# Attention into a dense pair on one core: all loads uncast in one ordered queue, casts on the engines, q and k as 96 rows of 6 tokens, pooling from the transposed copies

## Chip, cores, metric

The kernel runs on one NeuronCore of a Trainium2 chip. The metric is device time in microseconds (us), smaller is better. Times are medians over several executions; the kernel before takes 394.83 us (394.24 to 395.02, three runs).

Engine names: PE is the matmul engine (PEld its weight loads), DVE the vector engine, ACT the scalar engine, POOL the GpSimd engine, SP the engine that here only issues DMAs.

## The reference, cut to what matters

```python
# q, k, v: (8 batches, 8 heads, 576 tokens, 64), fp32; w_in (512, 2048), w_out (2048, 512)
q_d = q.reshape(B, H, 144, 4, D).mean(axis=3)       # the same for k_d, v_d
out_d = softmax(q_d k_d^T / 8) v_d                  # 144 x 144 scores
out_up = repeat(out_d, 4, axis=tokens)
out_local = softmax(mask(q k^T / 8)) v              # mask: |i - j| < 4
x = (out_up + out_local) as (4608 tokens, 512)
h = x @ w_in
out = (h - tanh(h)) @ w_out                         # fp32
```

For each head, q and k are needed twice: token by token, with the head dimension on the partitions, for a band of local scores, and averaged over groups of 4 tokens for the pooled scores. The attention output feeds two dense products, which are most of the PE's work.

## The kernel before

Words used below. A *pair* is two heads of one batch (128 columns of x). There are 32 pairs, four a batch. A *dense block* is 512 tokens of x; there are 9, each with 16 groups of four w_in matmuls (`mm1`) and 16 groups of four w_out matmuls (`mm2`). Block 0 needs all four pairs of batch 0, and so the first dense matmul cannot start before those four pairs are done.

The order of instructions on every engine is fixed when the kernel is built. Each step is recorded as an `op(engine, modelled ns, function, reads, writes, pri)`, and a list scheduler plays the steps through a model with those durations and emits them in the order that the model started them. Engines then run in that order.

```python
# scheduler, the choice of the next step on each engine
now = max(free.get(eng, 0.0), min(at[i] for i in cand))
pick = min((self.ops[i][4], i) for i in cand if at[i] <= now)[1]   # lowest pri first
# [cut]

def load_qk(p):                       # two casting DMAs a pair, issued by POOL: 128 rows of 4 tokens
    # [cut]
            GP.dma_start(out=qkn[s][:, i, hh:hh + 2],               # bf16 <- fp32 in DRAM
                in_=src[b, h0:h0 + 2, 0:512, :].rearrange("h (g a) d -> g h (a d)", a=4))
def load_tail(b):                     # tokens 512..575 of all heads: two more casting DMAs a batch
    # [cut]
def load_v(p):                        # fp32, SP's queue; windows of 128 tokens every 120 tokens
    # [cut]                           # rows of 64 floats (256 bytes)
def load_w(src, dst, name, f, pri):   # weights: four casting DMAs each, issued by POOL
    # [cut]
def prep_v(p):                        # POOL casts v into vw
    # [cut]

def attention(p):
    for i in range(2):                # DVE: put the tokens of q, k in order for the transposes
        op("DVE", 240, ...)           # qr <- qkn, bf16
    op("POOL", 1100, add1, ...)       # pooling on the loaded rows: a sum of token pairs,
    op("POOL", 650, add2, ...)        # then of the two sums
    def tr():                         # PE, one PSUM tile `ps`
        # 8 transposes 128x128, 1 transpose of the tail,
        # 2 matmuls for pooled q, k, and 1 that pools the tail
    # readers of that PSUM tile: ACT 512 columns of q, ACT 512 of k, ACT tails,
    #                            DVE pooled k (kd), ACT pooled q (qd)
    op("PE", 400, s1, reads=qks, writes=ts, pri=pri)   # first scores, into the same PSUM tile
    # [cut] exp, mask multiply, second scores (local window 4 and pooled), outputs, xT

def dense(kb):                        # kb 0: all mm1, then all mm2; kb 1: all mm1;
    # [cut]                           # then mm1 of block kb interleaved with mm2 of block kb - 1
```

The softmax here doesn't subtract the row's maximum and nothing guards it: scores larger than these inputs give would overflow.

Of the kernel before, what the change touches and what calls it, by code (L numbers as in the profile page):

```python
# [15 lines left out]
class Program:  # L16
# [34 lines left out]
    def order(self):  # L51
# [12 lines left out]
        for _ in range(n):  # L64
            best = None
            for eng, cand in ready.items():
                if not cand:
                    continue
                now = max(free.get(eng, 0.0), min(at[i] for i in cand))
                pick = min((self.ops[i][4], i) for i in cand if at[i] <= now)[1]  # L70
                if best is None or now < best[0]:
                    best = (now, eng, pick)
# [21 lines left out]
def kernel(  # L94
# [17 lines left out]
    SCALE = 1.0 / float(D) ** 0.5  # L112
    QW = 120
# [16 lines left out]
    NQKN, NVST, NVW = 3, 2, 3  # L130
    W_IN_PRI, W_OUT_PRI = -25, 0
# [7 lines left out]
    qkn = fixed("qkn", [128, 2, 4, 256], BF16, NQKN)  # L139
    tl = fixed("tl", [128, H * D], BF16, 2)  # L140
    vst = fixed("vst", [128, 4, NT, 64], FP32, NVST)
    vw = fixed("vw", [128, 4, NT, 65], BF16, NVW)
    vd = fixed("vd", [128, 2, 4, 65], BF16, NVW)
    qr = fixed("qr", [128, 2, 4, 128], BF16, 2)
    sm1 = fixed("half", [128, 2, 2, 128], BF16)
    sm = fixed("sm", [128, 2, 128], BF16, 2)
    qk = fixed("qk", [128, 1192], BF16, 2)
    qd = fixed("qd", [128, G], BF16, 2)
    kd = fixed("kd", [128, G], BF16, 2)
# [70 lines left out]

    def load_qk(p):

        b, h0, s = p // NP, 2 * (p % NP), (p // 2) % NQKN
        for i, src in enumerate((q, k)):
            key = ("qkn", s, p % 2, i)

            def issue(i=i, src=src):
                hh = 2 * (p % 2)
                GP.dma_start(
                    out=qkn[s][:, i, hh:hh + 2],  # L230
                    in_=src[b, h0:h0 + 2, 0:512, :].rearrange(
                        "h (g a) d -> g h (a d)", a=4))
            op("POOL", 700, issue, writes=[key, ("q", key)], pri=10 * p - 60)
            op("DMA", 1300, None, reads=[("q", key)], writes=[key],
               pri=10 * p - 60)

    def load_tail(b):
        for i, src in enumerate((q, k)):
            key = ("tl", b % 2, i)

            def issue(i=i, src=src):
                GP.dma_start(
                    out=tl[b % 2][64 * i:64 * i + 64, :].rearrange(
                        "p (h d) -> p h d", d=D),
                    in_=src[b, :, 512:576, :].rearrange("h p d -> p h d"))
            op("POOL", 750, issue, writes=[key, ("q", key)], pri=40 * b - 60)
            op("DMA", 1200, None, reads=[("q", key)], writes=[key],
               pri=40 * b - 60)

    def load_v(p):  # L250
        b, j = p // NP, p % NP
        hb = p // 2
        for hh in range(2):
            h, i = 2 * j + hh, 2 * (p % 2) + hh
            t = vst[hb % NVST]
            key = ("vst", hb % NVST, i)

            def win(tok, n, nt, base=v[b, h]):
                return bass.AP(tensor=base.tensor, offset=base.offset + tok * D,
                               ap=[[D, n], [QW * D, nt], [1, D]])  # L260

            def issue(h=h, i=i, t=t, win=win):
# [8 lines left out]
            if (b, h) in ((0, 0), (B - 1, H - 1)):  # L271
                def clear(h=h, i=i, t=t):
                    part = t[0:32, i, 0, :] if h == 0 else t[96:128, i, 4, :]
                    V.memset(part, 0.0)
                op("DVE", 100, clear, writes=[key], pri=-9)
            op("SP", 900, issue, writes=[key, ("q", key)], pri=10 * p - 55)
            op("DMA", 900, None, reads=[("q", key)], writes=[key], pri=10 * p - 55)

    def load_w(src, dst, name, f, pri):
        def issue():  # L280
            if src is moe_w_in:
                GP.dma_start(out=dst[:, :, 512 * f:512 * f + 512],
                             in_=src[:, 512 * f:512 * f + 512].rearrange(
                                 "(c p) f -> p c f", p=128))
            else:
                GP.dma_start(out=dst[:, 4 * f:4 * f + 4, :],
                             in_=src.rearrange("(f p) n -> p f n", p=128)
                             [:, 4 * f:4 * f + 4, :])
        key = (name, f)
        op("POOL", 800, issue, writes=[key, ("q", key)], pri=pri)  # L290
        op("DMA", 4500, None, reads=[("q", key)], writes=[key], pri=pri)


    def prep_v(p):
        hb, jj = p // 2, p % 2
        s, w = hb % NVST, hb % NVW
        pri = 10 * p - 52
        op("POOL", 650, lambda: GP.tensor_copy(
            out=vw[w][:, 2 * jj:2 * jj + 2, :, 0:64],
            in_=vst[s][:, 2 * jj:2 * jj + 2]),  # L300
           reads=[("vst", s, 2 * jj), ("vst", s, 2 * jj + 1)],
           writes=[("vw", w, jj)], pri=pri)

    def pool_v(hb):
# [11 lines left out]
        op("PE", 660, mm, reads=[("vw", w, 0), ("vw", w, 1), "pick"],  # L316
# [7 lines left out]
    def attention(p):  # L324
        b, j, hb, s, jj = p // NP, p % NP, p // 2, p % 2, p % 2
        tb, sn, w = b % 2, hb % NQKN, hb % NVW
# [4 lines left out]
        src = qkn[sn][:, :, 2 * jj:2 * jj + 2, :]  # L331


        for i in range(2):
            op("DVE", 240, lambda i=i: V.tensor_copy(  # L335
                out=qr[s][:, i].rearrange("p a (h d) -> p h a d", d=D),
                in_=src[:, i].rearrange("p h (a d) -> p h a d", d=D)),
               reads=[("qkn", sn, jj, i)], writes=[("qr", s, i)], pri=pri)

        def add1():  # L340
            with nc.allow_low_precision("pooled q and k"):
                GP.tensor_tensor(out=sm1, in0=src[:, :, :, 0:128],
                                 in1=src[:, :, :, 128:256], op=ALU.add)

        def add2():
            with nc.allow_low_precision("pooled q and k"):
                GP.tensor_tensor(  # L347
                    out=sm[s].rearrange("p i (h d) -> p i h d", d=D),
                    in0=sm1[:, :, :, 0:64], in1=sm1[:, :, :, 64:128], op=ALU.add)
        op("POOL", 1100, add1, reads=[("qkn", sn, jj, 0), ("qkn", sn, jj, 1)],  # L350
           writes=["sm1"], pri=pri - 57)
        op("POOL", 650, add2, reads=["sm1"], writes=[("sm", s)], pri=pri - 57)


        b16 = ps[:, 0].bitcast(BF16)
        t16 = ps[:, 1, 0:64].bitcast(BF16)
        g32 = ps[:, 1, 64:352]

        def tr():
            for i in range(2):  # L360
                for a in range(4):
                    c = 512 * i + 128 * a
                    T.transpose(b16[:, c:c + 128], qr[s][:, i, a, :], ident)  # L363
            tail = tl[tb][:, 128 * j:128 * j + 128]
            T.transpose(t16, tail, ident)
            for i in range(2):
                T.matmul(g32[:, G * i:G * i + 128], sm[s][:, i, :], ident,
                         start=True, stop=True)
            T.matmul(g32.rearrange("p (i g) -> p i g", i=2)[:, :, 128:144], tail,  # L369
                     group, start=True, stop=True)  # L370
        op("PE", 680, tr,
           reads=[("qr", s, 0), ("qr", s, 1), ("tl", tb, 0), ("tl", tb, 1),
                  ("sm", s), "ident", "group"], writes=ts, pri=pri)
        full = bass.AP(tensor=qk[s].tensor, offset=qk[s].offset,
                       ap=[qk[s].ap[0], [KOFF, 2], [1, 576]])
        for i in range(2):
            op("ACT", 480, lambda i=i: A.copy(  # L377
                out=full[:, i, 0:512].rearrange("p (g a) -> p g a", a=4),
                in_=b16[:, 512 * i:512 * i + 512].rearrange(
                    "p (a g) -> p g a", a=4)),  # L380
               reads=ts, writes=[("qk", s, i)], pri=pri)
        op("ACT", 170, lambda: A.copy(
            out=full[:, :, 512:576], in_=t16.rearrange("p (i c) -> p i c", i=2)),
           reads=ts, writes=[("qk", s, 2)], pri=pri)
        op("DVE", 230, lambda: V.tensor_copy(out=kd[s], in_=g32[:, G:2 * G]),
           reads=ts, writes=[("kd", s)], pri=pri)
        op("ACT", 190, lambda: A.activation(  # L387
            out=qd[s], in_=g32[:, 0:G], func=AF.Copy, scale=1.0 / 16.0),
           reads=ts, writes=[("qd", s)], pri=pri)
# [15 lines left out]
        def s2():  # L405
            for hh in range(2):
                score(4, hh, 128 + 384 * hh)
            for i in range(2):
                for hh in range(2):
                    rows = slice(64 * hh, 64 * hh + 64)  # L410
                    c = 224 + 384 * hh + G * i
                    T.matmul(sc[:, c:c + G], kd[s][rows, 16 * i:16 * i + 128],
                             qd[s][rows, :], start=True, stop=True)
        qks = [("qk", s, i) for i in range(3)]
        op("PE", 400, s1, reads=qks, writes=ts, pri=pri)
# [225 lines left out]
```

## Time and profile before

| | before |
|---|---|
| time, median | 394.83 us |
| span of the profiled run | 392.6 us |
| PE busy | 348.9 us (89%) |
| POOL busy | 151.0 us, 35.5 of it in the first 43 us |
| first dense matmul starts at | 43.1 us |
| software (casting) DMA / hardware DMA | 13.64 MB / 19.92 MB |

The page of the profile cuts the span into 40 slices of 9.8 us; a digit is the busy share of an engine in tenths. These are the rows of PE, POOL and PE's granted clock, and the two DMA queues:

```profile
...
PE   1466798976996899999999999999999999999996
...
POOL 8996654454769556645555322310000000000000
PEclk9997599998999799999999999999999999999999
...
q0 software_dynamic: 30080, 13.64, 28.2%
q1 hardware_dynamic: 47150, 19.92, 18.9%
...
```

PE is full from the fifteenth slice on, some 140 us; before that it has holes. POOL is the busiest engine of the first slices.

The same by stretches of the span. In each line: the stretch and its length, then the busy time and instruction count of each engine, the granted PE clock, the share of busy DMA engines and what they moved.

```profile
...
core 0: us, PE busy (x) PEld busy (x) DVE busy (x) ACT busy (x) POOL busy (x), PEclk, DMA share, GB/s
0.00:43.00 43.00, 19.59 (x216) 15.01 (x217) 21.76 (x50) 16.42 (x31) 35.49 (x59) 0.90 1.11 172
43.00:140.00 97.00, 83.54 (x749) 47.82 (x761) 63.34 (x118) 61.50 (x118) 58.70 (x74) 0.92 0.73 119
140.00:400.00 260.00, 245.72 (x1872) 128.70 (x1903) 143.85 (x251) 143.86 (x273) 56.79 (x71) 1.00 0.26 58
...
```

Span is PE's busy time plus its idle time, so PE's idle time says where the rest is: 43 - 19.59 = 23.4 us up to 43 us, 97 - 83.54 = 13.5 us between 43 and 140 us, and 252.6 - 245.72 = 6.9 us after it. (45 of 2,880 matmul records are missing in this trace. Between 43 and 140 us there are 12 fewer matmuls than weight loads, so at 0.216 us each idle time may be overstated there by 2.6 us.)

What POOL does in the first microseconds, in order of time (start, duration, engine, line, operation, tiles):

```profile
...
1.33 0.87 POOL L229 DMA_DIRECT2D qkn_71<-in_q_dram  x1 [0.81 <-POOLq L625]
...
2.91 0.72 POOL L242 DMA_DIRECT2D tl_74<-in_q_dram  x1
3.60 0.71 POOL L242 DMA_DIRECT2D tl_74<-in_k_dram  x1
...
6.19 0.73 POOL L229 DMA_DIRECT2D qkn_71<-in_k_dram  x1
7.08 1.17 POOL L342 TENSOR_TENSOR half<-qkn_71 128x512 bf16<-128x512 bf16 x1 [0.17 <-DMA qkn_71<-in_k_dram]
8.33 0.66 POOL L347 TENSOR_TENSOR sm_87<-half 128x256 bf16<-128x256 bf16 x1
...
9.59 0.61 POOL L207 TENSOR_SCALAR_AFFINE_SELECT mask<-mask 128x480 bf16<-128x480 bf16 x1
...
```

Each casting load costs POOL 0.7 to 0.9 us of issue, and pooling and the mask stand in line behind those. PE's first steps show what that does (in brackets the idle time before an instruction and what ended it):

```profile
...
9.70 0.26 PE L365 MATMUL ps_ts<-ident,tl_74 128*128 128x128 bf16 x1 [1.78 <-DMA tl_74<-in_k_dram]
...
12.34 0.58 PE L397 MATMUL ps_ts<-qk_89 64*128 64x120 bf16 x8 [2.14 <-ACT qd_91 L387]
...
43.10 0.58 PE L499 MATMUL ps_hy_497<-xT_65,w_in_sb 128*128 128x512 bf16 x1 [1.16 <-DVE xT_68 L479]
...
```

Eight transposes of pair 0 are through before 8 us, but the ninth, of the tail, waits for its tile until 9.70 us. Then the first scores wait 2.14 us, because they write the PSUM tile that five copies have to leave first; the pooled q (`qd`) is the last of the five. This wait comes again: in the whole span PE waits 8.2 us for `qd`.

```profile
...
PE ps_ts L397 <- ACT qd_91 L387: 4.5, 3, 2.1
...
PE ps_ts L397 <- ACT qd_92 L387: 3.7, 3, 2.1
...
```

### The profile page before, as it was taken

To read this page: it belongs to the slowest core of one execution; us is meant where nothing else is said; L and a number is where in the kernel's file an instruction comes from. 1 tells how busy PE (TensorE), PEld (TensorE's weight loads), DVE (VectorE), ACT (ScalarE), POOL (GpSimd) and SP (SyncE) were. 2 spreads that over 40 slices of the span, in tenths; PEclk is the share of its full clock that TensorE was granted. 3 is DMA by queue.
4 is the path that set the end of the run, shared out by engine and by line. 5 is a ranking of instruction groups with operands and counts; after the bars stand their busy time and mean duration, and the time that the engine had idled before them with its cause. 6 is when DMAs were issued, how large, how long until landed. Compare 5 with 4: busy or idle time off the path is not lost.

```text
span 392.6 us, 7296 instructions
## 1 busy us (share of the span) xinstructions
PE 348.9 (89%) x2835; PEld 191.5 (49%) x2880; DVE 228.9 (58%) x417; ACT 221.8 (56%) x421; POOL 151.0 (38%) x203
## 2 busy tenths in 40 slices
PE   1466798976996899999999999999999999999996
PEld 0345344444554565555655556555554444444442
DVE  3374487316897587777677766776644443343410
ACT  1536286364885677776776776767744444434421
POOL 8996654454769556645555322310000000000000
PEclk9997599998999799999999999999999999999999
DMA  9699993466759648568554400000010010101012
GB/s 158 126 185 209 203 186 63 60 116 128 130 92 154 116 64 139 95 132 138 96 110 69 66 29 23 33 2 28 28 53 28 28 53 28 53 27 45 37 53 80
DMA packets 77264, 34.02 MB, mean 87 GB/s; under 512 B 52142, under 2 KB 72622, under 8 KB 77230
## 3 DMA queue, kind: packets, MB, share of 16 engines
q0 software_dynamic: 30080, 13.64, 28.2%
q1 hardware_dynamic: 47150, 19.92, 18.9%
q8 instruction: 22, 0.36, 0.4%
q14 instruction: 12, 0.10, 0.1%
HBM read 37.74 MB, written 9.44 MB: 120 GB/s over the span
## 4 chain that ended last, share of the span: by engine, by line
PE 80%; ACT 8%; DVE 8%; issue 2%; DMA 2%; POOL 1%; ACTq 0%; DVEq 0%; POOLq 0%
PE ps_hy_497 L499 8%; PE ps_hy_498 L524 8%; PE ps_hy_499 L499 8%; PE ps_hy_499 L524 8%; PE ps_hy_500 L499 8%; PE ps_hy_500 L524 7%; PE ps_hy_497 L524 7%; PE ps_hy_498 L499 7%; PE ps_ts L397 3%; PE ps_ts L363 3%; PE ps_ox L444 2%; PE ps_ox L312 2%; ACT qk_89 L377 2%; ACT qk_90 L377 2%; PE ps_ox L474 2%
## 5 line engine op out<-in xcount | busy, mean ns | idle before, releaser
L499 PEld LDWEIGHTS <-w_in_sb 128*128 128x128 bf16 x576 | 53.8, 99 | 63.2 <-issue 6.1
L524 PEld LDWEIGHTS <-gT_103 128*128 128x128 bf16 x320 | 29.2, 97 | 32.7
L524 PEld LDWEIGHTS <-gT_104 128*128 128x128 bf16 x256 | 24.0, 98 | 27.1
L377 ACT COPY qk_89<-ps_ts 128x512 bf16<-128x512 bf16 x32 | 17.7, 591 | 25.6 <-PE ps_ts L369 24.6
L377 ACT COPY qk_90<-ps_ts 128x512 bf16<-128x512 bf16 x28 | 15.5, 590 | 15.8 <-PE ps_ts L369 14.1
L524 PE MATMUL ps_hy_498<-w_out_sb,gT_103 128*128 128x512 bf16 x79 | 20.0, 379 | 0.0
L524 PE MATMUL ps_hy_500<-w_out_sb,gT_103 128*128 128x512 bf16 x78 | 19.6, 379 | 0.4 <-issue 0.3
L524 PE MATMUL ps_hy_497<-w_out_sb,gT_103 128*128 128x512 bf16 x75 | 19.5, 379 | 0.3
L524 PE MATMUL ps_hy_499<-w_out_sb,gT_103 128*128 128x512 bf16 x76 | 19.4, 379 | 0.2
L347 POOL TENSOR_TENSOR sm_88<-half 128x256 bf16<-128x256 bf16 x16 | 11.2, 701 | 19.8 <-PE ps_ts L369 18.8
L347 POOL TENSOR_TENSOR sm_87<-half 128x256 bf16<-128x256 bf16 x16 | 12.0, 747 | 17.8 <-PE ps_ts L369 16.8
L363 PE MATMUL ps_ts<-ident,qr_84 128*128 128x128 bf16 x128 | 11.0, 234 | 7.6 <-DVE qr_84 L335 6.7
L460 DVE TENSOR_TENSOR ln_99<-ps_ox,r_97 128x896 bf16<-128x896 f32 x16 | 17.4, 1086 | 0.3
L416 ACT ACTIVATE E_95<-ps_ts 128x960 bf16<-128x960 f32 x16 | 15.6, 976 | 3.4 <-PE ps_ts L397 3.4
L420 DVE TENSOR_TENSOR E_95<-E_95,mask 128x960 bf16<-128x960 bf16 x16 | 12.4, 776 | 8.2 <-ACT E_95 L416 8.0
L416 ACT ACTIVATE E_96<-ps_ts 128x960 bf16<-128x960 f32 x14 | 13.6, 974 | 6.1 <-PE ps_ts L397 6.1
L397 PE MATMUL ps_ts<-qk_89 64*128 64x120 bf16 (+1 forms) x160 | 9.9, 219 | 7.7 <-ACT qd_91 L387 4.5
L524 PE MATMUL ps_hy_500<-w_out_sb,gT_104 128*128 128x512 bf16 x61 | 15.8, 379 | 0.4 <-issue 0.2
L524 PE MATMUL ps_hy_498<-w_out_sb,gT_104 128*128 128x512 bf16 x62 | 16.0, 379 | 0.1
L524 PE MATMUL ps_hy_497<-w_out_sb,gT_104 128*128 128x512 bf16 x61 | 15.9, 379 | 0.1
L524 PE MATMUL ps_hy_499<-w_out_sb,gT_104 128*128 128x512 bf16 x60 | 15.6, 379 | 0.3 <-issue 0.3
L460 DVE TENSOR_TENSOR ln_100<-ps_ox,r_98 128x896 bf16<-128x896 f32 x14 | 15.2, 1087 | 0.3
(227 smaller groups left out, 964.8 us busy)
## 6 DMA issues: line engine op xcount, KB each, us to landing
vst_76<-in_v_dram SPq DMA_DIRECT2D x31, 160.0 KB, 3.0
vst_77<-in_v_dram SPq DMA_DIRECT2D x31, 160.0 KB, 4.3
out_dram<-y_108 SPq DMA_DIRECT2D x12, 256.0 KB, 2.1
out_dram<-y_109 SPq DMA_DIRECT2D x12, 256.0 KB, 2.0
out_dram<-y_110 SPq DMA_DIRECT2D x12, 256.0 KB, 2.0
w_in_sb<-in_moe_w_in_dram POOLq DMA_DIRECT2D x4, 512.0 KB, 8.9
w_out_sb<-in_moe_w_out_dram POOLq DMA_DIRECT2D x4, 512.0 KB, 12.5
qkn_71<-in_q_dram POOLq DMA_DIRECT2D x12, 128.0 KB, 3.4
```

Of the source, the lines that this page charges most:

```text
L312: T.matmul(pv[:, 0, :], pick[:, t, :], vw[w][:, :, t, 0:64], start=(t == 0), stop=(t == NT - 1))
L347: GP.tensor_tensor(out=sm[s].rearrange("p i (h d) -> p i h d", d=D), in0=sm1[:, :, :, 0:64], in1=sm1[:, :, :, 64:128], op=ALU.add)
L363: T.transpose(b16[:, c:c + 128], qr[s][:, i, a, :], ident)
L377: op("ACT", 480, lambda i=i: A.copy(out=full[:, i, 0:512].rearrange("p (g a) -> p g a", a=4), in_=b16[:, 512 * i:512 * i + 512].rearrange( ...
L397: T.matmul(sc[:, c:c + NQ[t]], qk[s][rows, k0:k0 + 128], qk[s][rows, QW * t:QW * t + NQ[t]], start=True, stop=True)
L416: op("ACT", 870, lambda: A.activation(out=E[s][:, 0:960].rearrange("p (h c) -> p h c", h=2), in_=ps[:, :, 0:480], func=AF.Exp, scale=SCALE ...
L420: op("DVE", 760, lambda: V.tensor_tensor(out=E[s][:, 0:960].rearrange("p (h c) -> p h c", h=2), in0=E[s][:, 0:960].rearrange("p (h c) -> p ...
L444: T.matmul(po[:, hh, 65 * t:65 * t + 65], E[s][:, c:c + 128], vw[w][:, 2 * jj + hh, t, :], start=True, stop=True)
L460: op("DVE", 1010, lambda: V.tensor_tensor(out=ln[s].rearrange("p n (h d) -> p h n d", d=D), in0=blocks[:, :, :, 0:64], in1=r[s].unsqueeze( ...
L474: T.transpose(px[0][:, QW * t:QW * t + n], ln[s][0:n, t, :], ident[0:n, 0:n])
L499: T.matmul(ps_hy[slot], w_in_sb[:, dc, fc * 128:(fc + 1) * 128], xT[dc][:, kb * 512:kb * 512 + 512], start=(dc == 0), stop=(dc == N_DC - 1))
L524: T.matmul(ps_hy[slot], gT[g][:, fc, ts * 128:ts * 128 + 128], w_out_sb[:, fc, :], start=(fc == 0), stop=(fc == N_FF - 1))
```

## The change

Its intent: take the 88 load issues off POOL, start earlier, and give PE less to do in each pair.

1. All loads go uncast (fp32) through SP's one hardware queue, in the order of the program. The Trainium skill ("DMA: Bandwidth & Descriptors", SWDGE vs HWDGE vs iDMA) says that a DMA that casts has to be issued by GpSimd; the two queue lines above agree with it, 13.64 MB. So the casts move to engines.
2. q and k are loaded as 96 rows of 6 tokens. That covers all 576 tokens, and the tail goes. 12 transposes of 96 columns replace 9 of 128 and 3 pooling matmuls.
3. Pooling reads the transposed copies `qk` (DVE in batch 0, POOL after it).
4. The weights are staged as fp32 in buffers that are idle early (gT, and xT's later half) and cast by POOL, ACT and DVE.
5. Eight of block 0's sixteen `mm2` groups are kept as filler for block 1.

The diff, cut to its core:

```diff
+                if eng == "DMA":                      # the queue serves in order of arrival
+                    pick = min((at[i], i) for i in cand)[1]
+    def load(ns, fn, keys, cost, pri):
+        op("SP", ns, fn, writes=list(keys) + ["queue", ("q", keys[0])], pri=pri)
+        op("DMA", cost, None, reads=[("q", keys[0])], writes=keys, pri=pri)
     def load_qk(p):
-                GP.dma_start(out=qkn[s][:, i, hh:hh + 2],
-                    in_=src[b, h0:h0 + 2, 0:512, :].rearrange("h (g a) d -> g h (a d)", a=4))
-            op("POOL", 700, issue, ...)
+                nc.sync.dma_start(out=qkn[s][:, i], in_=src[b, h0:h0 + 2].rearrange(
+                        "h (g a) d -> g h (a d)", a=A6))            # A6 = 6
+            load(500, issue, [("qkn", s, i)], T_QK, -30)
-    def load_tail(b): [cut]
     def load_v(p):
+            load(1000, issue, [("vst", s, i)], T_V, -30)
     def load_w(...):
+        load(600, issue, keys, T_W, -30)                            # fp32 into idle buffers
+        for c in range(4):
+            op(eng, ns, lambda ...: fn(out=to, in_=part), ...)      # casts: POOL, ACT, POOL, DVE
     def attention(p):
+            op(eng, ns, ... fn(out=dst, in_=srt) ...)    # reorder and cast: DVE, and ACT or POOL
+                for a in range(A6):
+                    T.transpose(b16[:, G6 * a:G6 * a + G6], qr[s][:, i, a, :], ident[0:G6, 0:G6])
-        # tail transpose, pooling matmuls, copies of kd and qd
+        op(e2, ..., half <- four[..., 0:2] + four[..., 2:4], reads=[("qk", s, 0), ("qk", s, 1)])
+        op(e2, ..., qkd <- half[..., 0] + half[..., 1])
     def dense(kb):
+            for i in range(M2_FIRST): mm2(kb, i)         # the other 8 go between block 1's mm1
+    M2_FIRST = 8
+    T_QK, T_V, T_W, W_PRI, NEARLY = 1000, 550, 2900, -3, NP
```

`T_QK` and `T_V` are the modelled times of one q or k load and of one v load.

## The prediction

> **What bounds the kernel now.** From about 140 us it is TensorE: busy time by stretches gives 245.7 of 249 us between 140 and 389. The losses are early. From 0 to 43.1 us, when the first dense matmul starts (timeline of PE), PE is busy only 19.6 us, at half pace; the chain of waits there runs through DVE, ACT, POOL and a DMA. Between 43 and 140 us PE idles another 13 us, at a clock of 0.93 and 0.91. The timeline shows why: POOL is busy 35.5 of the first 43.1 us, issuing cast-loads (0.73 us each), pooling (1.16 + 0.7 us a pair) and building the mask. Pair 0 waits for the tail tile until 9.7 us; the first PSUM copy is at 10.2, the first exp at 13.0. While POOL works, DVE's reorder copies grow from 0.28 to 0.75-1.44 us.
>
> **What the change does.**
> - Takes 88 load issues from POOL. The Trainium skill ("DMA: Bandwidth & Descriptors", SWDGE vs HWDGE vs iDMA) says a cast in a DMA must take the GpSimd path; so casts move to engines. POOL gains, per later pair, a k reorder (estimate 0.9 us, from the 640-element cast at 0.75) and pooling that now follows the copies (estimate 1.3 + 0.8, scaled by size): 2 us of new latency before the second scores, which dense work should hide.
> - PE: 12 transposes of 96 columns replace 9 of 128 and 3 pooling matmuls: 0.65 us a pair (warm) becomes an estimated 0.52, 4 us in all, on the critical path.
> - ACT: two copies of 576 (estimate 0.65 each) replace 1.77 us. DVE: one reorder of 0.8 replaces 1.0 plus a 0.31 cast. In the first batch DVE takes the pooling (1.1 us a pair) and ACT the k reorder (0.74).
> - 32 weight casts of about 0.5 us, 16 inside the first batch, at fixed places of in-order engines: late weights block attention behind them.
> - q0 can land near 4 us instead of 5.5, and no tail is waited for: the first PSUM copy near 6, not 10.2.
>
> **Sum.** With four pairs of about 13 us chain, two at a time, and DVE and ACT needing some 24 and 20 us for the first batch, I expect the first dense matmul at 34 us (30 to 38) instead of 43: 9 us. PE work saves 4 us. Bubbles and half-pace stretches between 43 and 140 us (about 20 us lost) should shrink by 5 to 7, because loads run ahead and half of dense block 0's second matmul is kept as filler. Total about 19 us: **375 us**, range **365 to 386**. Chances: faster by over 2% 0.90, within 2% 0.07, slower 0.03.
>
> **What would show it.** First dense matmul before 38 us; first exp near 8-9; no software DMA traffic in the queue table; transposes at 0.042 us each when warm; first w_out matmuls near 53 us instead of 65; PE idle in the first stretch down by 8-10 us; from 140 us still over 98% PE.
>
> **What would make it wrong.** (1) The one queue is slower than I think: 8 MB of fp32 weights are ordered between batches. At 250 GB/s w_in lands at 35 us and w_out at 66, casts block ACT and DVE, and most of the gain goes; v's 256-byte rows issued at about 1 us each under load before, so this is the main risk. (2) DVE and POOL still slow each other. (3) The longer pooling chain stalls PE where there is little dense work. (4) The order is fixed by modelled durations; where they are off, an engine waits. If everything flows as planned, the first dense matmul comes at 29 us and the time is near 366.

## More of the kernel before

A wrong modelled duration costs nothing by itself, but the order that it leads to is obeyed: an instruction whose data is late holds up all instructions behind it on its engine.

## The result

| | before | after |
|---|---|---|
| time, median (range), four runs each | 394.92 us (394.24 to 396.2) | 379.69 us (378.52 to 380.0) |
| span of the profiled run | 392.6 us | 378.2 us |
| PE busy | 348.9 us | 342.2 us |
| POOL busy | 151.0 us | 114.6 us |
| first dense matmul | 43.1 us | 36.1 us |
| first w_out matmul | 65.4 us | 59.8 us |

The ratio is 0.9605 (95% interval 0.9573 to 0.9637). Here and below a ratio is the mean time of one kernel's fast runs over that of the kernel before in the same rounds, so it is not quite the ratio of the medians that are quoted.

The lines of the page that answer to those of before, with the row of DMA rates, one number a slice:

```profile
...
PE   2675989849999999999999999999999999999995
...
POOL 5144565445345433445434543223000000000000
PEclk9965899978999999999999999999999999999999
...
GB/s 195 238 384 209 193 366 242 206 212 264 152 99 160 140 151 125 127 127 141 159 149 127 126 125 30 30 28 29 29 28 32 53 28 56 29 28 57 28 55 83
...
q1 hardware_dynamic: 64782, 47.19, 51.0%
...
```

The software queue is gone. In its first ten slices the rate row has two kinds: 366 to 384 GB/s where a weight passes, and some 190 to 270 in the slices of q, k and v. The stretches:

```profile
...
0.00:43.00 43.00, 25.21 (x254) 16.39 (x256) 26.67 (x61) 24.67 (x42) 18.08 (x37) 0.80 1.10 249
43.00:140.00 97.00, 86.19 (x838) 47.88 (x849) 64.68 (x109) 64.12 (x120) 46.54 (x58) 0.96 0.86 201
140.00:400.00 260.00, 230.76 (x1744) 119.82 (x1775) 130.74 (x204) 133.37 (x240) 50.03 (x57) 1.00 0.24 67
...
```

PE's idle time is now 17.8 us up to 43 us, 10.8 us between 43 and 140 us, and 238.2 - 230.76 = 7.4 us after it. So the 14.4 us of span come from PE's busy time (6.7), its first 43 us (5.6) and the stretch to 140 us (2.7); after 140 us nothing is won (0.6 is lost). Of the 6.7 us, some 3.9 are saved work (see below); where the rest comes from was not traced.

The early part is mended as meant: pair 0's transposes start at 4.36 us and the first scores at 8.01 us, after 0.73 us of waiting for a copy.

```profile
...
4.36 0.66 PE L341 MATMUL ps_ts<-ident,qr_87 96*128 96x96 bf16 x6 [4.36 <-DVE qr_87 L330]
...
8.01 0.58 PE L371 MATMUL ps_ts<-qk_89 64*128 64x120 bf16 x8 [0.73 <-ACT qk_89 L345]
...
```

Two spots are not. The first is the start of the dense work:

```profile
...
33.99 0.66 PE L341 MATMUL ps_ts<-ident,qr_87 96*128 96x96 bf16 x6 [0.95 <-DVE qr_87 L330]
35.66 0.66 PE L341 MATMUL ps_ts<-ident,qr_87 96*128 96x96 bf16 x6 [1.01 <-POOL qr_87 L330]
36.12 0.63 PE L473 MATMUL ps_hy_519<-xT_65,w_in_sb 128*128 128x512 bf16 x1
...
```

The last xT of batch 0 ended at 34.6 us (33.86 + 0.74), but the transposes of pair 4, of the next batch, stand ahead of the dense matmuls in PE's order and wait twice for their data, about 1 us each. So the first dense matmul comes at 36.12 us, 1.5 us late. It also starts at half clock: until 39.66 us the dense matmuls start 0.43 us apart and the granted clock is 0.50. Those of the kernel before start 0.43 us apart too, from 43.10 us on.

The second is larger, at 80 us. PE, then POOL, in order of time:

```profile
...
80.26 0.22 PE L371 MATMUL ps_ts<-qk_89 64*128 64x96 bf16 x2
84.14 0.42 PE L386 MATMUL ps_ts<-qkd_92 64*128 64x144 bf16 x4 [3.66 <-POOL qkd_92 L360]
84.49 0.61 PE L473 MATMUL ps_hy_521<-xT_65,w_in_sb 128*128 128x512 bf16 x1
84.89 0.64 PE L473 MATMUL ps_hy_521<-xT_66,w_in_sb 128*128 128x512 bf16 x1
...
```

```profile
...
80.75 0.72 POOL L291 CAST vw_83<-vst_80 128x640 bf16<-128x640 f32 x1 [3.63 <-DMA vst_80<-in_v_dram]
81.41 0.82 POOL L330 CAST qr_87<-qkn_73 96x768 bf16<-96x768 f32 x1
82.20 1.14 POOL L354 TENSOR_TENSOR half<-qk_89 128x576 f32<-128x576 bf16 x1
83.42 0.67 POOL L360 TENSOR_TENSOR qkd_92<-half 128x288 bf16<-128x288 f32 x1
...
```

PE waits 3.66 us for the pooled q and k (`qkd_92`) of the current pair. POOL could have made them earlier, but in its order a cast of v (`vw_83`), for a later pair, comes first, and it waits 3.63 us for a DMA. The chain of waits confirms it: in it the wait for `vst_80` is 8.28 us long and ends at 80.62 us. After the stall, matmuls start 0.40 to 0.43 us apart instead of 0.216. The Trainium skill ("TensorE: Matmul & The Clock Gate", Part 1) says that the clock falls to half after an idle window of about 3.4 us, and gives 426.7 and 215.7 ns for 512 columns; this stall agrees with both, with a wait of 3.66 us and a granted clock of 0.50 from 84 to 88 us. But so long a wait was not needed everywhere in this trace: in the 10 us before the half-clock start at 36.12 us no wait of PE was longer than 1.47 us.

Why the DMA was late: the model gave one pair 2 x 1.0 us for q and k and 2 x 0.55 us for v, 3.1 us in all. The loads of batch 1 took about 19 us for four pairs, 4.7 us each. The queue is thus behind its schedule until about 85 us, and every instruction whose place was chosen by the model may stand too early.

### The profile page after: what moved, and what is told of

The parts are those of the page before. It is cut to its first block, busy times and chain, and to the rows that moved or that the text cites. A ratio compares the mean times of both kernels' runs of the same rounds, so it can differ in the third digit from the quotient of the medians.

```text
span 378.2 us, 7323 instructions
## 1 busy us (share of the span) xinstructions
PE 342.2 (90%) x2832; PEld 184.1 (49%) x2880; DVE 222.1 (59%) x371; ACT 222.2 (59%) x401; POOL 114.6 (30%) x151
## 4 chain that ended last, share of the span: by engine, by line
PE 65%; DMA 14%; ACT 5%; DVE 5%; SPq 4%; issue 3%; POOL 3%; POOLq 0%; ACTq 0%; DVEq 0%
PE ps_hy_519 L498 8%; PE ps_hy_521 L498 7%; PE ps_hy_519 L473 6%; PE ps_hy_521 L473 6%; PE ps_hy_522 L498 6%; PE ps_hy_522 L473 6%; PE ps_hy_520 L473 6%; PE ps_hy_520 L498 6%; DMA vst_80<-in_v_dram 5%; DMA gT_102<-in_moe_w_in_dram 3%; SPq L256 3%; PE ps_ts L341 2%; DMA qkn_72<-in_k_dram 2%; DMA gT_103<-in_moe_w_out_dram 2%; PE ps_ts L371 2%
## 5 line engine op out<-in xcount | busy, mean ns | idle before, releaser
L473 PEld LDWEIGHTS <-w_in_sb 128*128 128x128 bf16 x576 | 52.4, 99 | 58.6 <-issue 3.9
L498 PEld LDWEIGHTS <-gT_102 128*128 128x128 bf16 x320 | 30.4, 98 | 35.6
L498 PEld LDWEIGHTS <-gT_103 128*128 128x128 bf16 x256 | 24.2, 98 | 28.1
L345 ACT COPY qk_89<-ps_ts 128x576 bf16<-128x576 bf16 x32 | 19.5, 645 | 15.2 <-PE ps_ts L341 15.2
L345 ACT COPY qk_90<-ps_ts 128x576 bf16<-128x576 bf16 x28 | 16.7, 643 | 9.5 <-PE ps_ts L341 9.5
L341 PE MATMUL ps_ts<-ident,qr_87 96*128 96x96 bf16 x192 | 13.0, 219 | 8.6 <-DVE qr_87 L330 5.3
L354 POOL TENSOR_TENSOR half<-qk_89 128x576 f32<-128x576 bf16 x14 | 16.6, 1189 | 8.2 <-ACT qk_89 L345 8.2
L354 POOL TENSOR_TENSOR half<-qk_90 128x576 f32<-128x576 bf16 x14 | 16.3, 1162 | 9.4 <-ACT qk_90 L345 9.4
L341 PEld LDWEIGHTS <-qr_87 96*128 96x128 bf16 x192 | 10.4, 104 | 10.3 <-DVE qr_87 L330 5.5
```

Source lines behind the costliest of these rows:

```text
L341: T.transpose(b16[:, G6 * a:G6 * a + G6], qr[s][:, i, a, :], ident[0:G6, 0:G6])
L345: op("ACT", 540, lambda i=i, b16=b16: A.copy(out=full[:, i].rearrange("p (g a) -> p g a", a=A6), in_=b16.rearrange("p (a g) -> p g a", a=A6)),
L354: op(e2, 1150 if e2 == "POOL" else 700, lambda: eng.tensor_tensor(out=half, in0=four[:, :, :, 0:2], in1=four[:, :, :, 2:4], op=ALU.add), r ...
L473: T.matmul(ps_hy[slot], w_in_sb[:, dc, fc * 128:(fc + 1) * 128], xT[dc][:, kb * 512:kb * 512 + 512], start=(dc == 0), stop=(dc == N_DC - 1))
L498: T.matmul(ps_hy[slot], gT[g][:, fc, ts * 128:ts * 128 + 128], w_out_sb[:, fc, :], start=(fc == 0), stop=(fc == N_FF - 1))
```

## The experiments

The main theory (called Q) was that the slow queue, with the order made for a faster one, took back a part of the gain. Rivals were that POOL had become too slow for pooling (P), that DVE and ACT bounded the first batch (D), that the weights' staging hurt, that the filler was what helped, and that the loads alone, or the rows and pooling alone, were the gain. One more question was how much of PE's saved work was worth time at all. All diffs are against the changed kernel, if not told otherwise.

| label | change | time, median | ratio to before | 95% interval |
|---|---|---|---|---|
| (after) | | 379.69 | 0.9605 | 0.9573 to 0.9637 |
| e1_v_long_rows | v in long rows (wrong result) | 371.11 | 0.9414 | 0.9363 to 0.9464 |
| e2_v_cast_later | v cast behind pooling | 371.98 | 0.9428 | 0.9391 to 0.9465 |
| e3_queue_as_measured | order made for 4.7 us a pair | 368.76 | 0.9348 | 0.9307 to 0.939 |
| e4_weights_cast_dma | weights by casting DMA | 375.79 | 0.9526 | 0.9485 to 0.9568 |
| e5_dense_order_old | no filler | 376.83 | 0.9526 | 0.9452 to 0.96 |
| e7_both_orders | e2 and e3 | 368.06 | 0.9328 | 0.9278 to 0.9378 |
| e8_before_uncast_qk | before, q and k uncast | 392.81 | 0.9977 | 0.9904 to 1.0049 |
| e9_four_more_transposes | PE work added | 381.2 | 0.967 | 0.9608 to 0.9733 |
| e11_long_rows_both_orders | e1 and e7 (wrong result) | 368.69 | 0.9319 | 0.926 to 0.9377 |
| e12_both_orders_old_dense | e7, no filler | 371.13 | 0.9382 | 0.9332 to 0.9432 |
| e6_before_new_dense_order | before, with filler | 397.82 | 1.0066 | 0.9997 to 1.0135 |
| e13_qk_cast_dma | e7, q and k by casting DMA | 376.25 | 0.9531 | 0.95 to 0.9562 |

### e1_v_long_rows: is the queue's rate a limit?

Its output is wrong, which doesn't matter for the time. v's rows hold other tokens than they should.

```diff
-   nc.sync.dma_start(out=t[:, i], in_=win(-4, 128, 5))          # 640 rows of 256 bytes
+   nc.sync.dma_start(out=t[:, i]....[:, 0:288],                 # 128 rows of 1,152 bytes
+       in_=bass.AP(tensor=base.tensor, offset=base.offset, ap=[[288, 128], [1, 288]]))
```

> Wrong result on purpose: v is read as 128 rows of 1152 bytes (10% fewer bytes, 4.5 times fewer rows), everything else and the engines' orders kept. Theory Q (the load queue limits the first 85 us, and the 256-byte rows of v are its slow part): q/k/v phases move well over 200 GB/s (near the 366 of the weight phases), the wait of PE for the pooled q/k at 84 us (3.7 us, plus 1.7 at half clock) goes, first dense matmul moves from 36.1 to 33 or 34, time 371 to 375. Rival P (POOL's pooling chain is too slow by itself) and rival D (DVE and ACT bound the first batch): unchanged within 1.5 us, 378 to 380.

Measured: 371.11 us, first dense matmul at 32.54 us. What the DMA queues moved from 30 to 37 us, when both kernels load only q, k and v, first in the changed kernel, then here:

```profile
...
DMA packets 2677, 1.40 MB, mean 200 GB/s; under 512 B 2115, under 2 KB 2667, under 8 KB 2676
...
```

```profile
...
DMA packets 1307, 1.65 MB, mean 235 GB/s; under 512 B 123, under 2 KB 1306, under 8 KB 1306
...
```

The rate rises, and as a pair is 885 KB here (two heads of q, k and v) it takes 3.8 us by this rate, instead of 4.7. So v's short rows held the queue back. But the expectation missed in two points: the rate is far from that of the weights, and the wait at a late v cast is still there (3.0 us, now at 75 us). This run changes the rate and, with it, every arrival, so it does not say yet whether the rate or the order is to blame.

### e2_v_cast_later: take the v cast out of the way

```diff
-           reads=[("vst", s, 0), ("vst", s, 1)],
+           reads=[("vst", s, 0), ("vst", s, 1)] + ([("qkd", p % 2)] if p > 3 else []),
 [...]
-        if p + 2 < NPAIR:
-            prep_v(p + 2)
         attention(p)
+        if p + 2 < NPAIR:
+            prep_v(p + 2)
```

The added dependency makes the model place the cast of a later v behind the current pair's pooling.

> The changed kernel, but POOL's cast of a later pair's v is placed behind the pooling of the current pair, so a late v cannot hold up pooled q/k. Loads, engines and amounts of work are the same. Theory Q with in-order blocking: the 3.7 us wait at 84 us and the half-clock stretch after it shrink by at least 3 us in all, time 374 to 377. Rival P (pooling of 1.15 + 0.67 us is itself too long): the wait stays, 378 to 380.

Measured: 371.98 us, 7.7 us less than the changed kernel and better than expected. The first dense matmul stays at 36.29 us. The stretches from 60 us show the cure:

```profile
...
60.00:80.00 20.00, 16.62 (x171) 9.47 (x172) 11.90 (x18) 9.98 (x20) 10.03 (x13) 1.00 1.19 203
80.00:100.00 20.00, 19.84 (x201) 11.36 (x203) 15.13 (x26) 15.70 (x30) 7.84 (x10) 1.00 1.16 239
...
```

PE is busy 19.84 of 20 us between 80 and 100 us. In the changed kernel that stretch reads:

```profile
...
80.00:100.00 20.00, 16.22 (x148) 8.60 (x149) 10.68 (x19) 10.92 (x20) 11.54 (x14) 0.83 0.90 207
...
```

So the stall also cost clock (0.83 against 1.00). POOL has the same work and the same speed as before the edit (busy 114.8 us, and 114.6 in the changed kernel); it only does it in another order. PE's longest wait for `qkd` falls from 3.66 to 0.9 us. This refutes P.

### e3_queue_as_measured: only a number of the model

```diff
-    T_QK, T_V, T_W, W_PRI, NEARLY = 1000, 550, 2900, -3, NP
+    T_QK, T_V, T_W, W_PRI, NEARLY = 1000, 1350, 2900, -3, NP
```

With 1.35 us a v load, the model gives a pair 2 x 1.0 + 2 x 1.35 = 4.7 us, as measured. Nothing that the chip does is changed but the order.

> The changed kernel with one constant of its scheduler changed: a v load is taken as 1350 ns instead of 550, near what the saturated queue showed (about 4.7 us for a pair's q, k and two v). Only the engines' fixed orders change. Theory Q with wrong order: the transposes of pair 4 no longer stand in front of the first dense matmul (36.1 to about 34.7), the wait at 84 us goes, time 372 to 376. If the order costs nothing (queue rate alone, or rival D): 378 to 381.

Measured: 368.76 us, 10.9 us less than the changed kernel, again more than expected. The first dense matmul:

```profile
...
32.74 0.58 PE L473 MATMUL ps_hy<-xT,w_in_sb 128*128 128x512 bf16 x1 [1.20 <-DVE xT L453]
...
```

It now waits for xT alone: it is the 217th matmul in PE's order instead of the 229th, ahead of pair 4's transposes. From 60 to 100 us PE is busy 39.25 of 40 us. Theory Q holds in this form: not the slow queue but an order made for a faster one. Rival D, which expected 378 to 380 us, falls as the reason for the lost time; what the first dense matmul still waits for, though, is DVE.

### e7_both_orders: do the two cures add up?

The edits of e2 and e3 together.

> The changed kernel with both order edits: a v load taken as 1350 ns by the scheduler, and POOL's cast of a later v behind the current pooling. Correct result. If both cure the same blocking, the time is that of the better alone, 367 to 370; if they add, 361 to 365.

Measured: 368.06 us. Alone the two were worth 7.7 and 10.9 us; together they are worth 11.6 and not 18.6, so the two largely cure the same blocking. The intervals of e3 and e7 overlap. This is the best correct version (ratio 0.9328), and not to be told from e3.

```profile
...
0.00:43.00 43.00, 26.76 (x268) 16.84 (x271) 27.72 (x63) 26.48 (x46) 17.38 (x36) 0.84 1.09 255
43.00:140.00 97.00, 92.23 (x952) 53.48 (x967) 72.63 (x120) 71.23 (x135) 56.34 (x64) 0.96 0.98 218
140.00:400.00 260.00, 220.14 (x1616) 112.98 (x1643) 119.14 (x190) 123.08 (x223) 45.74 (x52) 1.00 0.21 60
...
```

PE's idle time between 43 and 140 us is down to 4.8 us (10.8 in the changed kernel; this trace lacks 15 matmul records there, so 4.8 may be overstated by 3.2).

### e11_long_rows_both_orders: the rate again, with an order that fits

e1's rows in e7. The result is wrong.

> Wrong result on purpose: v in long rows as in the first experiment, together with both order edits. If the rate of the queue still costs time once the order fits the arrivals: 361 to 365 (3 us or more below the 368 of both order edits alone). If the rate was only costly because the fixed order expected the data earlier: 366 to 370, no gain left.

Measured: 368.69 us, as e7. With the order of the changed kernel, faster rows were worth 8.6 us; with an order that fits the arrivals, nothing. So this step of the rate, from 200 to 235 GB/s, was worth time only through the order.

### e4_weights_cast_dma: the weights as before

```diff
-        load_w(moe_w_in, w_in_sb, "w_in", f, *stages[f])
+        load_w(moe_w_in, w_in_sb, "w_in", f, -21, ("vst", 3, 1))     # POOL, casting, after batch 0's v
 [...]
-                    load_w(moe_w_out, w_out_sb, "w_out", f, *stages[2 + f])
+                    load_w(moe_w_out, w_out_sb, "w_out", f, 19, ("vst", 1, 1))
```

> One part undone: weights are loaded by cast DMAs from POOL as before, issued after the first batch's v (w_in) and the second batch's v (w_out); q, k, v stay on the SP queue. If the gain came from staged weights: back to 385 or more. Theory Q: the same bytes pass the same engines, 16 casts leave DVE, ACT and POOL in the first batch, so first dense 34 to 36 if w_in lands in time, total 376 to 383.

Measured: 375.79 us, just under the expected range and faster than the changed kernel by 0.8% in the ratio, though the first dense matmul comes at 36.68 us (expected 34 to 36) and the first w_out matmul only at 69.99 us. So staging is not where the gain came from. More can't be said: the edit also gives the model another order, and an accident of the order is worth as much as this (see e5 and e12).

### e5_dense_order_old, e12_both_orders_old_dense and e6_before_new_dense_order: the filler

```diff
-    M2_FIRST = 8
+    M2_FIRST = 16          # e5: in the changed kernel; e12: in e7
```

e6 is the reverse: the kernel before with the new `dense`.

> The changed kernel with one part undone: all of dense block 0's second matmuls come straight after its first ones again (the constant M2_FIRST 16 instead of 8), so none is kept as filler for block 1. If the filler is worth what I gave it in the prediction (part of 5 to 7 us): 381 to 384. If PE between 60 and 100 us is starved by the load queue anyway, filler only moves the gap: 378 to 381.

> Both order edits, and dense block 0's second matmuls all straight after its first (M2_FIRST 16). Correct result; candidate for the best version. With the wrong order the filler cost 3 us (376.8 against 379.7); if that was the filler itself: 364 to 366; if it was an accident of that order: 367 to 371.

> The kernel before with only the change's dense order (8 of block 0's 16 second matmul groups kept back as filler for block 1). If the filler helps where it has stalls to fill: 389 to 393 (before has about 20 us of idle and half-clock time between 43 and 140 us). If it does nothing or harm, as in the changed kernel: 394 to 398.

Measured: 376.83 us for e5 (the expectation of 378 to 384 missed), 371.13 us for e12 (just above the upper end of its expectation) against e7's 368.06, and 397.82 us for e6 against 395.77 of the kernel before. Without the filler the changed kernel is a little faster, the well-ordered one a little slower, and the filler doesn't help the old kernel; in all three comparisons the intervals overlap or hold 1. So no worth of the filler is shown, and its sign goes with the order, some 3 us either way; it is not the source of the gain.

### e8_before_uncast_qk: the loads alone

Against the kernel before: q, k and the tail come as fp32 through SP, the tail is cast by ACT, and the weights stay casting DMAs, issued after the first batch's v.

```diff
-                GP.dma_start(out=qkn[s][:, i, hh:hh + 2], ...       # bf16, POOL
+                nc.sync.dma_start(out=qkn[s][:, i, hh:hh + 2], ...  # fp32, SP
+        op("ACT", 620, lambda: A.copy(out=tl[b % 2], in_=tf[b % 2]), ...)
```

> The kernel before with one part of the change: q, k and the tail are loaded uncast over the SP queue (fp32 tiles; the reorder copies and the poolings read fp32, the tail gets one cast a batch on ACT); old rows of 4 tokens, old pooling, weights still cast by POOL's DMAs, w_in issued after the first batch's v. Theory: POOL's load issues and the late tail are what made the start slow, so the first dense matmul comes at 37 to 40 us instead of 43 and the time is 386 to 391. If the gain of the start came from the new rows and the pooling instead: first dense 42 to 44, time 392 to 396.

Measured: 392.81 us, the same as before. The first dense matmul comes at 37.59 us, 5.5 us earlier, as expected; the time expected with it (386 to 391) does not come. PE's idle time is 4.4 us shorter than before up to 43 us, but 1.3 us longer from there to 140 us and 0.9 us longer after it. One stretch in which PE starves:

```profile
...
110.00:120.00 10.00, 7.80 (x100) 5.05 (x99) 7.48 (x15) 6.68 (x14) 5.11 (x6) 0.98 0.60 161
120.00:130.00 10.00, 7.07 (x46) 4.55 (x48) 6.32 (x10) 5.26 (x10) 4.73 (x5) 0.51 0.61 160
...
```

PE is busy 14.9 of these 20 us, and the second ten run at half clock (0.51 granted). But the kernel before stalls there too, so this stretch alone does not say where the early start was lost. There it reads:

```profile
...
110.00:120.00 10.00, 9.79 (x109) 5.96 (x109) 9.90 (x19) 7.61 (x16) 8.52 (x11) 1.00 0.68 87
120.00:130.00 10.00, 5.75 (x81) 4.56 (x79) 6.85 (x12) 5.26 (x11) 8.84 (x11) 0.81 0.89 160
...
```

DVE, which now reads fp32, is busy 240.9 us in all instead of 228.9, and the waits for the last copy of the PSUM tile (`qd`) are still 7.0 us. Here the early start was worth nothing that can be measured, since PE is not kept fed after it. No run gives these loads an order made for them, so whether they would pay with one is open.

### e13_qk_cast_dma: all but the loads of q and k

```diff
-                nc.sync.dma_start(out=qkn[s][:, i], ...             # e7: fp32, SP
+                GP.dma_start(out=qkn[s][:, i], ...                  # bf16, POOL casts in the DMA
+            op("POOL", 700, issue, writes=[key, ("q", key)], pri=10 * p - 60 if p > 1 else -100)
```

> The complement of the run that gave the old kernel the uncast q and k loads alone (no gain there): the best version so far (both orders, 368.1 us), but with q and k loaded by POOL's casting DMAs again as bf16 rows of 6 tokens, two issues of about 0.7 us a pair, first pair ahead of POOL's constants; weights and v stay uncast in the one queue. Theory 'combination' (rows and pooling gain only together with the uncast loads, because POOL's 45 us of issues come back and slow DVE): 384 to 395 us, first dense matmul after 38 us. Rival 'rows and pooling alone carry it' (shorter PE work, scores that wait for two copies only): 368 to 376 us. In between, 376 to 384: both parts count. POOL busy should go from about 115 to about 160 us; the profile should show DVE's copies slower.

Measured: 376.25 us, ratio 0.9531 (five rounds). It is 0.25 us above the range of the theory that rows and pooling carry all, and well below that of the theory that they gain only with the loads. The second falls; both parts count, with rows and pooling (and the order) the larger. The first dense matmul, and the stretches:

```profile
...
41.13 1.86 PE L475 MATMUL ps_hy<-xT,w_in_sb 128*128 128x512 bf16 x4 [0.68 <-DVE xT L455]
...
```

```profile
...
0.00:43.00 43.00, 21.57 (x234) 14.70 (x236) 23.94 (x56) 21.85 (x37) 28.65 (x53) 0.83 1.07 253
43.00:140.00 97.00, 92.18 (x891) 50.13 (x892) 70.95 (x116) 68.31 (x128) 62.98 (x83) 0.99 0.66 136
...
```

The dense work starts at 41.13 us, only 2 us earlier than before. PE is then busy 92.18 of the 97 us to 140 us; it was 83.54 in the kernel before. (This trace misses no matmul record, so its idle time is not overstated as the others' is.) POOL is busy 157.8 us, as the kernel before was (151.0); after 43 us that costs PE little. DVE's copies, expected slower, are faster: a reorder takes 0.36 us on average between 40 and 140 us, from bf16, and 0.75 in e7, from fp32. Against e7 the run lacks 8.2 us, and its dense work starts 8.6 us later: here the earlier start was worth about its length.

### e9_four_more_transposes: is PE's saved work worth time?

```diff
-                for a in range(A6):
+                for a in list(range(A6)) + ([4, 5] if p >= NP else []):
```

Four transposes more in each of 28 pairs, written twice to the same place with the same data: the result stays correct.

> The changed kernel with 4 redundant transposes of 96 columns a pair (the same blocks written again) in the 28 later pairs; order unchanged. They are worth 28 x 4 x 0.043 = 4.8 us of PE. If PE work in these pairs is on the critical path one for one: 384 to 385. If half of it hides in PE's gaps: 381.5 to 382.5.

Measured: 381.2 us, ratio 0.967. PE's busy time grows by 3.8 us, the span by 1.5 us, and the ratio by 0.0065, about 2.6 us of 394. That would put some 40 to 70% of PE work in the attention part on the critical path. But the intervals overlap, and the noise of the two ratios (0.006 and 0.003 either way) is as large as the difference: neither none nor all of the 3.8 us is ruled out. The time is just under the 381.5 to 382.5 us expected if half of the work hides.

## Why the prediction was right, and where it was not

The time came out within the range, 4.7 us above the estimate of 375. The parts:

- *First dense matmul at 34 us (30 to 38).* It came at 36.12 us; 7.0 us of the 9 us arrived. PE's idle time up to 43 us fell by 5.6 us, where the prediction looked for 8 to 10. 1.5 us of the rest are pair 4's transposes that stand first in PE's order; e3 moves them and starts at 32.74 us. The mechanism was right: POOL's busy time in the first 43 us fell from 35.5 to 18.1 us, and no tail is waited for. The first PSUM copy was predicted near 6 and came at 5.96 us; the first exp, predicted at 8 to 9, at 10.4 us.
- *PE work saves 4 us, on the critical path.* The work was sized right: in a quiet stretch the transposes and pooling matmuls of a pair took 0.80 us end to end before (154.02 to 154.82 us) and take 0.68 us after, and 32 times 0.12 is 3.9 us. "On the critical path" is not shown to the full: e9 points to 40 to 70% of such work there, within a noise that rules out neither none nor all.
- *Bubbles between 43 and 140 us shrink by 5 to 7 us, "because loads run ahead and half of dense block 0's second matmul is kept as filler".* This is the step that failed. PE's idle time there fell by 2.7 us, from 13.5 to 10.8. Neither cause that the prediction gave is true: loads do not run ahead, the queue is behind until about 85 us, and no run shows a worth of the filler (e5, e6, e12). What is missing is mainly the stall at 80 us (3.66 us); e2 and e3 take it away, and idle time falls to 6.7 us in e2 and 4.8 us in e3 and e7.
- *Risk (1), a queue slower than thought that blocks engines, was named as the main risk,* and it is what happened, though with another victim. The prediction feared the weights. Their first casts came at 22.4 to 32.1 us, and the first dense matmul never waited for them. It was v's casts on POOL that blocked, by way of risk (4), an order fixed by modelled durations that were off: e3 changes one such duration and nothing else. Risk (3), the longer pooling chain, is not what stalled PE at 80 us (e2). The first w_out matmul came at 59.8 us and not near 53, without a wait in front of it: the order had put it there.
- *A benefit not foreseen:* the first scores now wait for two copies of the PSUM tile instead of five. The waits for `qd` (8.2 us) are gone, and the waits for `qk` in their place are 2.2 us.

So where did the gain come from? Rows and pooling, together with a fitted order, staged weights and filler but without the uncast loads of q and k, are worth 4.7% (e13); the loads alone on the old kernel 0.2% (e8, not to be told from nothing); on top of the rest 2% more (e7 against e13). The changed kernel got 4.0% of these 6.7%, because its order was made for a queue of 3.1 us a pair.

Left open: how the gain of e13 splits between the rows of 6 tokens and the pooling from copies. The tail, the PSUM tile and the pooling hang together, and no run parts them. Nor does any run give the kernel before, or e8, an order made for measured durations, so how much of e13's 4.7% is due to its order is not shown. What staging the weights costs or gains by itself is open too, since e4's order differs as well.

## What to carry to other kernels

Where engines run in a fixed order, the modelled durations decide what blocks what: measure the queue under its real load and put that number into the model, since here this one number (0.55 to 1.35 us) was worth 10.9 us. Don't put a cast of later data ahead of the current chain on an in-order engine, unless the data is surely there. And an earlier start pays only if what follows can keep the bounding engine fed: such loads were worth nothing measurable in the old kernel (e8) and 8 us in the new one (e7 against e13), each in its own order.

## What the Trainium skill lacked or had wrong

- "DMA: Bandwidth & Descriptors", Specifications, puts the smallest transfer for line rate at 512 bytes, and the limit of memory at some 358 GB/s. Here rows well above 512 bytes were far from it: e1's stretch from 30 to 37 us holds rows of 1,152 and 1,536 bytes, all but 123 of 1,307 packets are over 512 bytes, the DMA engines were busy, and it moved 235 GB/s. The weights' rows of 2,048 bytes moved at 366 to 384 GB/s, also where a load was of 256 KB only (382 GB/s from 56 to 58 us), so it isn't the size of one load. Whether the row's length or the 96 partitions of q and k make the difference, no run tells.
- The same page speaks of back-pressure only for DMAs between cores. Here SP's issue of a local load took 0.38 us for the first load of the program (at 0.81 us) and 2.57 us with others ahead of it (at 18.63 us), and loads issued between 30 and 52 us took 7.7 to 9.5 us to land (medians by tile).
- "TensorE: Matmul & The Clock Gate", Part 4, gives a transpose about 275 ns in a kernel and says that full clock doesn't engage for it. As the duration of one that is near what is seen here (0.22 us on average for 96 columns), but among other matmuls they overlap: twelve take 0.68 us end to end at a granted clock of 1.00, so they start some 42 ns apart, and adding 112 (e9) took 3.8 us of PE's busy time, 34 ns each. So where the dense matmuls around them hold the clock up, transposes run at it too; what they do to the clock alone no run tells.
- "SBUF — State Buffer", Who interferes with whom, says that DVE and GpSimd share a port pair as an exclusive lock and the loser blocks. This agrees with the trace: a mask multiply of DVE takes 0.65 us alone; one that began at 70.41 us, while POOL's cast (until 70.61 us) and then its add (70.58 to 71.72 us) ran, ended at 72.24 us, as if it had waited for both. What the page has no number for is how much that costs in a kernel: e13 brought 38 us of POOL's work back (157.8 us against e7's 119.5), and DVE's mask multiplies between 40 and 140 us grew only from 0.80 to 0.99 us on average.
